# Weight words by ScalarE, dilated heads in three tiles of 128 rows, and a new order list in an attention and feed-forward kernel

## The chip, the core and the metric

The kernel runs on one core of one Trainium2 chip. The metric is the device time of one execution in microseconds; the time of a kernel is the median of its runs. Five engines work beside one another, each through its own list of instructions: TensorE (PE, with PEld for its weight loads), VectorE (DVE), ScalarE (ACT), GpSimd (POOL) and SyncE (SP), whose list here issues nearly all transfers between HBM and on-chip memory.

## The reference

Two stages, one behind the other. Attention over 8 batches, 8 heads, 576 positions and a head dimension of 64, in which each query sees at most 32 keys: in heads 0 to 3 ("plain") the 32 latest positions, in heads 4 to 7 ("dilated") 32 positions at a distance of 4.

```python
mask_plain = (rel >= 0) & (rel < 32)
mask_dil = (rel >= 0) & (rel < 128) & (rel % 4 == 0)
attn = softmax(where(mask, q @ k.T / sqrt(64), -1e9))     # + 1e-9 in the denominator
x = (attn @ v).transpose(0, 2, 1, 3).reshape(4608, 512)
h = x @ w_in                                              # 512 -> 2048
out = (h * tanh(log1p(exp(h)))) @ w_out                   # 2048 -> 512
```

All arrays are float32, and the matrices arrive as pairs of 32-bit words.

## The kernel before, in words

**Units.** The work is cut into 16 units, a batch and a half of its positions each: 288 tokens, all eight heads. For each unit the attention's output x is written transposed into one tile of 512 rows in four chunks and multiplied by both matrices. Matrices, x and the gated values are split into a high and a low fp16 part, and products of parts are summed in PSUM.

**Direct units and late units.** Units 0 to 2 are "direct": their attention runs in float32, the probabilities and x are transposed by TensorE (`transpose_p` L659, `transpose_x` L738), and the second matrix is multiplied in full by `ff2` (L972). Units 3 to 15 are "late": probabilities and values are split in fp16 parts (three passes), transposed by DMA, and the second matrix goes through a scheme with seven products in place of eight (`product`, L933, 144 columns). The first matrix is `ff1` (L790, 288 columns) in all units; Mish is an activation into `hm` and a few operations of ScalarE and VectorE.

**Attention on TensorE.** Queries are cut into blocks of 32, and a block meets only its window of 64 keys (32 before it and its own), so each small matmul uses 64 rows by 32 columns of TensorE. Plain heads: three tiles of three blocks, on 96 partitions. Dilated heads: the positions of each of the four residues modulo 4 are a tile of three blocks that overlap a little, on 96 partitions, thus four tiles. `scores_of_kind` (L577) writes scores of one kind of head, `scores` subtracts maxima, `exps` takes the exponential, `values` (L689) multiplies by v with a column of ones for the denominator. The four dilated tiles don't fit into one PSUM bank at once, so `values` runs for them twice, `va.1` and `va.2`, with two tiles each, and `transpose_x` as well.

**Weights.** Each matrix is loaded in groups (`w_load`; in the list `wl`), as words in four buffers `raw`. `w_max` (`wm`) copies the high words for the maximum: by ScalarE for w_in, by GpSimd for w_out (the set `BY_POOL`). `w_words` (`ww`) builds float32 from the two words in three steps: a scaled low half by GpSimd (L411), then two word operations of VectorE (L413, L415). `w_scale` (`ws`) finds a power of two with matmuls by a matrix of ones, and `w_split` (`wp`) makes the high part by ScalarE (L422) and the low part by VectorE (L424).

**Order.** Every engine's order is fixed by one list, `ORDER`. Each word names a step and its unit or group (`ld1` the loads of q and k of unit 1, `lv1` of its v, `qp1` GpSimd's copy of its q, `sp` scores, `sc` maxima, `ex`, `tp`, `va`, `tx` as above, `pr` scales of v, `ff0.6` a chunk of ff1, `fo` of ff2, `fs` scales of ff1). A step is a generator: each time its word comes up, the part up to the next `yield` is issued. "=2" names the PSUM bank, of four, that the step takes. `kw` and `kh` are matmuls whose result nobody reads. In `loads_v` of a direct unit the dilated v comes in one transfer for each third of a residue (`vd`, 128 KB); they write parts of one tile, and each waits on SP for the one ahead of it.

Of the kernel before, what the change touches and what calls it, by code (L numbers as in the profile page):

```python
# [51 lines left out]
ww1.1.0 pr1 va1.2 ff0.2 ww0.2.0 va1.2 va1.0 ws0.2=3 ww0.2.0 ff0.2 ff0.3=1 ws0.2 tx1.2=2 ld2 tx1.2 ff0.3 wp0.2.0
va1.0 wp0.2.1 tx1.0=3 tx1.2 wp0.2.0 wp0.2.1 sp2.1=0 wm1.1.0 va1.1=2 sp2.1 ff0.3 wl1.1.1 va1.1 tx1.0 tx1.0 ff0.5=1
ww1.1.1 va1.1 sc2.1 ff0.4=3 wm1.1.1 qp2 ft wl1.0.0 wl1.0.1 fs0.4 fs0.2 va1.1 ww1.1.0 wm1.0.0 ff0.5 ff0.4 tx1.1=0 fs1
sp2.0=2 ff0.5 ww1.1.1 tx1.1 tx1.1 ff0.4 sp2.0 gt0.0=0 ff1.0=1 gt0.1=1 lv2 sc2.0 ws1.1=0 ww1.1.1 ww1.0.0 ff1.6=3
ws1.1 lv2 ff1.7=2 ex2.0 ff1.7 wp1.1.1 wp1.1.1 gt0.2=2 gt0.0 ff1.0 ff1.2=0 gt0.3=3 gt0.3 ld3 ex2.1 ff1.6 wm1.0.1 lv2
# [1005 lines left out]
```

## Time and profile before

| what | value |
|---|---|
| median of 3 runs | 858.7 us (857.71 to 860.95) |
| the profiled execution | 862.81 us, of which the profile's span is 860.9 |
| mean granted clock of TensorE | 0.992 |
| TensorE busy | 842.1 us (98% of the span) |
| VectorE busy | 636.1 us (74%) |
| ScalarE busy | 477.8 us (55%) |
| GpSimd busy | 96.0 us (11%) |
| read and written in HBM | 56.89 MB and 9.44 MB |

The span begins at the first and ends at the last instruction of the program; the rest of the profiled execution's own time lies around it. Busy time is the union of an engine's instructions. The matmuls' ends are modelled, so a busy TensorE says that it had matmuls in flight, not that it worked at its peak.

### The profile page before, as it was taken

Reading aid. Unit: us, or ns where it says so; the run is one execution under the profiler, and the core shown is the slowest. Engines: PE = TensorE matmul, PEld = TensorE weight load, DVE = VectorE, ACT = ScalarE, POOL = GpSimd, SP = SyncE. Lnnn points to the kernel's source line nnn. Section 1 sums busy time; section 2 is a strip of 40 time slices with the busy share of each in tenths; the row PEclk is TensorE's granted clock in tenths of the full one; section 3 lists DMA queues with packets and bytes.
Section 4 is the critical chain, followed back from the end, with each engine's and each line's share of the span. In section 5 each row is a group of like instructions: output and inputs, shape, how many; then the busy total and the mean of one; then the engine's idle time right before and its main releaser. Section 6 shows DMA issues by size and latency. Waiting matters only on the chain.

```text
span 860.9 us, 32197 instructions
## 1 busy us (share of the span) xinstructions
PE 842.1 (98%) x14818; PEld 727.3 (84%) x14821; DVE 636.1 (74%) x818; ACT 477.8 (55%) x615; POOL 96.0 (11%) x99
## 2 busy tenths in 40 slices
PE   8798999999999999999999999999999999999998
PEld 7486777788788998988999889988889889988898
DVE  3788998586999897968777587977878764854353
ACT  2464655453486558765753775766446656624342
POOL 5116583210010001000000000010000000000000
PEclk9989999999999999999999999999999999999999
DMA  8648543366320437253623373725335160421001
GB/s 270 213 151 266 154 146 87 73 144 130 70 57 13 126 80 178 57 144 96 126 67 102 69 150 76 131 72 102 94 73 109 43 127 18 57 40 34 1 22 37
DMA packets 154887, 86.29 MB, mean 100 GB/s; under 512 B 92288, under 2 KB 150656, under 8 KB 154752
## 3 DMA queue, kind: packets, MB, share of 16 engines
q1 hardware_dynamic: 154752, 84.24, 40.9%
q8 instruction: 116, 1.90, 1.0%
q14 instruction: 19, 0.16, 0.1%
HBM read 56.89 MB, written 9.44 MB: 77 GB/s over the span
## 4 chain that ended last, share of the span: by engine, by line
PE 86%; DMA 7%; DVE 3%; SPq 2%; ACT 1%; issue 1%; POOL 0%; DVEq 0%; POOLq 0%; ACTq 0%
PE b L790 40%; PE b L933 31%; PE b L972 8%; DMA vf<-in_vd 4%; PE b L689 4%; PE b L577 3%; DMA raw<-in_w_in 2%; DMA knd<-in_kdT 1%; DVE g L903 1%; SPq L348 1%; DVE hm L909 0%; DVE w L424 0%; SPq L501 0%; PE b L385 0%; ACT g L901 0%
## 5 line engine op out<-in xcount | busy, mean ns | idle before, releaser
L790 PE MATMUL b<-x,w 128*128 128x288 f16 x3072 | 393.4, 286 | 0.2 <-ACT hm L796 0.2
L790 PEld LDWEIGHTS <-w 128*128 128x128 f16 x3072 | 295.4, 98 | 75.5 <-issue 0.6
L903 DVE SCALAR_TENSOR_TENSOR g<-hm,sg,g 128x1152 f16<-128x1152 f32 (+1 forms) x104 | 131.3, 1272 | 53.7 <-ACT g L901 52.9
L933 PE MATMUL b<-g,w 128*128 128x144 f16 x2496 | 164.9, 226 | 0.8 <-issue 0.7
L933 PEld LDWEIGHTS <-w 128*128 128x128 f16 x2496 | 158.4, 98 | 3.2 <-issue 1.1
L796 ACT ACTIVATE hm<-b,fs 128x576 f32<-128x576 f32 x128 | 92.8, 738 | 113.5 <-PE b L790 99.2
L901 ACT ACTIVATE g<-hm,sg 128x1152 f16<-128x1152 f32 (+1 forms) x104 | 116.0, 1127 | 40.1 <-PE b L933 26.4
L481 POOL COPY qp<-qn 128x576 f32<-128x576 f32 x15 | 34.9, 2326 | 433.6 <-DMA qn<-in_qT 317.9
L909 DVE TENSOR_TENSOR hm<-hm 128x576 f32<-128x576 f32 x104 | 79.0, 763 | 1.9 <-ACT hm L796 0.4
L972 PE MATMUL b<-g,w 128*128 128x288 f16 x576 | 73.3, 286 | 0.1
L947 ACT ACTIVATE y<-b,fo 128x288 f32<-128x288 f32 x52 | 40.6, 786 | 58.9 <-PE b L933 57.6
L972 PEld LDWEIGHTS <-w 128*128 128x128 f16 x576 | 55.6, 98 | 14.4 <-DVE w L424 0.3
L952 DVE SCALAR_TENSOR_TENSOR y<-b,fo,y 128x144 f32<-128x144 f32 x78 | 33.6, 478 | 45.8 <-PE b L933 22.7
L933 PE MATMUL b<-g,g 128*128 128x144 f16 x936 | 66.6, 226 | 0.3 <-DVE y L952 0.2
L933 PE MATMUL b<-g,late_sums 128*128 128x144 f16 x936 | 65.9, 226 | 0.0
L933 PEld LDWEIGHTS <-g 128*128 128x128 f16 x936 | 60.6, 98 | 2.2 <-issue 0.6
L933 PEld LDWEIGHTS <-late_sums 128*128 128x128 f16 x936 | 60.0, 98 | 0.5
L727 ACT CAST x<-xs 96x512 f16<-96x512 f32 (+1 forms) x39 | 26.7, 686 | 30.9 <-DMA x<-x 17.1
L729 DVE TENSOR_TENSOR x<-xs,x 96x512 f16<-96x512 f32 (+1 forms) x39 | 30.1, 772 | 16.6 <-ACT x L727 16.4
L545 DVE SCALAR_TENSOR_TENSOR vh<-vn,s,vh 128x2688 f16<-128x2688 f32 (+1 forms) x13 | 35.2, 2705 | 8.6 <-ACT vh L543 8.6
L705 DVE TENSOR_TENSOR xs<-b,rec 96x512 f32<-96x512 f32 (+1 forms) x48 | 37.2, 776 | 4.4 <-DVE rec L703 0.5
L689 PEld LDWEIGHTS <-pT 64*32 64x32 f16 (+1 forms) x3276 | 30.2, 90 | 5.3 <-issue 3.6
(127 smaller groups left out, 821.1 us busy)
## 6 DMA issues: line engine op xcount, KB each, us to landing
qn<-in_qT SPq DMA_DIRECT2D x15, 576.0 KB, 5.3
vn<-in_vd SPq DMA_DIRECT2D x66, 128.0 KB, 3.8
raw<-in_w_out SPq DMA_DIRECT2D x16, 512.0 KB, 5.2
out_T<-y SPq DMA_DIRECT2D x26, 288.0 KB, 2.8
raw<-in_w_in SPq DMA_DIRECT2D x12, 512.0 KB, 7.4
vn<-in_v SPq DMA_DIRECT2D x14, 288.0 KB, 4.2
knd<-in_kdT SPq DMA_DIRECT2D x14, 224.0 KB, 4.7
vn<-in_v SPq DMA_DIRECT2D x12, 256.0 KB, 3.7
```

What stands on the lines that cost most here:

```text
L481: nc.gpsimd.tensor_copy(qp.rearrange("p (b r i) -> p b r i", r=NR, i=SQ // NR), d["q"][:, :2 * HT].rearrange("p (b i r) -> p b r i", r=NR, ...
L545: nc.vector.scalar_tensor_tensor(lo, src, s, hi, ALU.mult, ALU.subtract)
L689: nc.tensor.matmul(avv[s * SQ:(s + 1) * SQ, a, t - t0, h * (D + 1):(h + 1) * (D + 1)], p, vv[vi][ks, v0:v0 + D + 1], start=(i == 0), stop= ...
L705: nc.vector.tensor_tensor(xs.rearrange("p (a t h e) -> p a t h e", a=2, h=2, e=D), avv[:, :, :, 1:AW - 1].rearrange("p a t (h e) -> p a t ...
L790: nc.tensor.matmul(ph[:, h, :HT], w1[j][:, c, wi, k * P:(k + 1) * P], x_of(d, xi, c), start=(n == 0), stop=(n == len(seq) - 1))
L796: nc.scalar.activation(d["m"][p][:, half, k0:k0 + 2], ph[:, :, :HT], AF.Mish, scale=d["fs"][:, j:j + 1])
L901: nc.scalar.activation(hi, src, AF.Identity, scale=sg)
L903: nc.vector.scalar_tensor_tensor(lo, src, sg, hi, ALU.mult, ALU.subtract)
L909: nc.vector.tensor_tensor(a, a, b, op=op)
L933: nc.tensor.matmul(acc[e], left(l, e, p, wi)[:, k * P:(k + 1) * P], right(gi, k), start=(n in opens and p == 0 and q == 0), stop=(last and ...
L947: nc.scalar.activation(into(half, t), by(acc), AF.Identity, scale=fo)
L972: nc.tensor.matmul(po[:, :HT], w2[:, e, j, wi, k * P:(k + 1) * P], d["g"][j][:, gi, k, :], start=(j == 0 and n == 0), stop=(j == NCH - 1 a ...
```

## The change

It does three things. The scaled low halves of all weight words and the copies for the maxima of w_out are made by ScalarE (`BY_POOL` is empty), none by GpSimd. The twelve dilated blocks of a unit lie in three tiles of four blocks, on 128 partitions, in place of four tiles of three on 96; `block` gives the residue and the third for a tile's place j, the tiles' widths follow from `QS` and `NB`, and one `values` and one `transpose_x` per kind remain (`va0.1`, `tx0.1`; there is no `va0.2`). And `ORDER` is a new list throughout, in which the same steps stand in another order and with other banks. Below, its first lines stand for the list.

```diff
 ORDER = """
-ld0 ld0 wl0.3.0 lv0 mf cs0 qp0 ww0.3.0 xa0 cs1 wl0.3.1 xa1 kw18 kh32 sp0.0=0 wm0.3.0 ld0 mf lv0 ww0.3.0 ld0 wm0.3.0
-wl0.0.0 wm0.3.1 lv1 ww0.3.0 sp0.0 wl0.0.1 ww0.3.0 ww0.3.1 kw17 sp0.1=1 sc0.0 ww0.0.0 sp0.1 ww0.3.0 ww0.3.1 lv0
-ww0.3.1 ws0.3=2 sc0.1 wm0.0.0 ws0.3 lv0 ww0.0.0 ww0.3.0 ld1 ww0.0.1 ww0.0.0 sc0.0 sc0.1 wm0.0.1 ex0.0 ld1 wp0.3.1
-kw8 tp0.0=3 ww0.0.1 wp0.3.1 kw1 ws0.0=2 ex0.1 ld1 ws0.0 ww0.0.1 qp1 wp0.0.0 tp0.1=0 kw3 sp1.0=1 tp0.1 sp1.0 ld1 lv0
-sp1.1=2 sp1.1 lv1 wp0.0.1 wl0.1.0 tp0.0 wp0.0.0 sc1.0 sc1.0 sc1.1 pr0 sc1.1 pr0 va0.0=0 wl0.1.1 wp0.3.0 pr0=3 pr0
-ex1.1 va0.0 va0.1=3 ww0.1.0 va0.0 wp0.3.0 va0.1 ex1.0 va0.2=2 lv1 va0.2 lv1 va0.0 va0.1 tp1.1=1 va0.1 wl0.2.1
-wm0.1.0 va0.2 fs0.0 tx0.1=3 va0.0 va0.2 wm0.1.1 tp1.1 kw1 tx0.0=0 ww0.1.0 tx0.1 ww0.1.1 lv1 tx0.0 tp1.0=2 ww0.1.1
-tp1.0 tx0.2=1 tx0.1 wl0.2.0 ws0.1=2 tx0.2 tx0.0 ld2 tx0.2 ww0.2.1 ff0.6=3 ff0.6 wp0.0.1 ws0.1 wm0.2.1 ww0.1.1
...
+wl0.3.0 wl0.3.1 lv0 ww0.3.0 kw12 wm0.3.0 wl0.0.0 ww0.3.0 wm0.3.0 lv0 cs0 ld0 wl0.0.1 ww0.3.0 wm0.3.1 wm0.0.0 ld0
+kh30 mf ww0.0.0 qp0 ld0 ww0.3.1 kw4 ww0.0.0 mf ld0 kw26 ww0.3.0 ww0.3.0 ww0.3.1 ws0.3=0 ww0.0.0 cs1 sp0.0=1 sp0.0
+ws0.3 sp0.1=2 wm0.0.1 sp0.1 ww0.0.1 ld1 xa1 qp1 lv0 lv0 ww0.0.1 sc0.0 sc0.0 ld1 ww0.3.1 ld1 sc0.1 ex0.0 ws0.0=3
+sc0.1 tp0.0=0 ex0.1 tp0.0 sp1.0=1 ld1 kw2 lv2 lv0 ws0.0 sp1.1=3 sp1.1 ww0.3.0 wp0.0.0 ww0.0.1 wp0.0.1 tp0.1=2 sc1.1
+wp0.3.0 sc1.1 wp0.3.0 wp0.3.1 wl0.1.1 va0.0=0 va0.0 pr0 tp0.1 pr0 sp1.0 va0.0 sc1.0 pr0=2 pr0 xa0 sc1.0 va0.1=2
+va0.1 va0.0 wp0.0.0 ex1.1 va0.1 va0.1 va0.0 va0.1 kw2 wl0.2.0 ex1.0 tx0.0=3 lv1 ww0.2.0 ld2 tx0.1=0 ld2 tx0.0
+wm0.2.0 tx0.1 tp1.0=1 qp2 wl0.1.0 wp0.0.1 wp0.3.1 tx0.0 ww0.1.1 lv1 wl0.2.1 tp1.1=2 lv1 wm0.1.0 tx0.1 ww0.1.0
+wm0.1.1 ff0.6=3 tp1.1 ff0.0=0 ww0.2.0 ff0.0 fs0.0 ww0.2.0 ff0.0 tp1.0 ww0.1.1 ww0.1.0 ff0.6 ws0.1=2 ff0.1=0 ff0.7=1
+ww0.1.0 lv1 ws0.1 fs0.3 wm0.2.1 ww0.1.1 ff0.1 ww0.2.1 ww0.2.1 wp0.1.0 ff0.6 wp0.1.0 ws0.2=2 ff0.7 wl1.0.0 sp2.0=3
...
-    NB = (NPB, NR)
+    NB = (NPB, NR * NS * SQ // P)
+    QS = (QB, P)
...
-    XW = 4 * HT + 4 * NR * QB
+    XW = 4 * (QS[0] * NB[0] + QS[1] * NB[1])
+    QMAX = max(QS)
+    GMAX = max(NB)
...
-    BY_POOL = {(1, g) for g in range(NCH)}
+    BY_POOL = set()
...
-    ident_b = const.tile([QB, QB], BF16, name="ident_b")
+    ident_b = const.tile([QB, 2 * QB], BF16, name="ident_b")
...
-            nc.gpsimd.tensor_scalar(lo[:, c], lo[:, c].bitcast(U32), LOW_SCALE, LOW_BIAS, ALU.mult, ALU.add)
+            nc.scalar.activation(lo[:, c], lo[:, c].bitcast(U32), AF.Copy, scale=LOW_SCALE, bias=LOW_BIAS)
...
+    def block(kind, t, j):
+
+        return divmod(t * P // SQ + j, NS) if kind else (t, j)
...
             for a in range(2):
-                for s in range(NS):
-                    k0 = a * (NR * d["kd"] if kind else d["kw"]) + key_of(d, kind, t, s)
-                    q0 = (2 + a) * HT + t * RB + s * DQ if kind else a * HT + t * QB + s * SQ
+                for j in range(nq // SQ):
+                    r, s = block(kind, t, j)
+                    k0 = a * (NR * d["kd"] if kind else d["kw"]) + key_of(d, kind, r, s)
+                    q0 = (2 + a) * HT + r * RB + s * DQ if kind else a * HT + t * QB + s * SQ
                     for h in range(2):
                         hs = slice(h * D, (h + 1) * D)
-                        c = (2 * t + a) * WK
+                        c = (2 * t + a) * w
                         q = d["q"] if kind else d["qp"]
-                        nc.tensor.matmul(pt[s * SQ:(s + 1) * SQ, h, c:c + w], q[hs, q0:q0 + SQ], d["k"][kind][hs, k0:k0 + w],
+                        nc.tensor.matmul(pt[j * SQ:(j + 1) * SQ, h, c:c + w], q[hs, q0:q0 + SQ], d["k"][kind][hs, k0:k0 + w],
                                          start=not d["direct"], stop=True, skip_group_check=True)
...
+        nb, w, nq = NB[kind], width_of(d, kind), QS[kind]
         n = 2 * nb
-        sb = d["sb", kind] = pool.tile([QB, 2 * NR * 2 * WK], F32, name="sb", bufs=2)
-        nm = pool.tile([QB, 2, 2 * NR], F32, name="nm", bufs=4)
-        src = pt[:QB, :, :n * WK].rearrange("p h (g k) -> p h g k", k=WK)[:, :, :, :w]
+        sb = d["sb", kind] = pool.tile([QMAX, 2 * GMAX * 2 * WK], F32, name="sb", bufs=2)[:nq]
+        nm = pool.tile([QMAX, 2, 2 * GMAX], F32, name="nm", bufs=4)[:nq]
+        src = pt[:nq, :, :n * w].rearrange("p h (g k) -> p h g k", k=w)
...
-    def span(p):
-
-        return (1, 2 * p - 2, 2 * p) if p else (0, 0, NPB)
-
-    def values(u, p):
-        d = U[u]
-        kind, t0, t1 = span(p)
+                nc.tensor.transpose(pt[:, h, t * nq:(t + 1) * nq], sb[:, g * P:(g + 1) * P], ident[:nq, :nq])
+        pp = d["p", kind] = early.tile([P, 2, nb * nq], F32, name=f"pp{kind}")
+        yield
+        nc.scalar.copy(pp, pt[:, :, :nb * nq])
+
+    def values(u, kind):
+        d = U[u]
         pp = d["p", kind]
-        nb, ng = NB[kind], 2 * (t1 - t0)
+        nb, nq = NB[kind], QS[kind]
         av = take("b", banks)
-        avv = av[:QB, :, :ng * (D + 1)].rearrange("p a (t e) -> p a t e", e=AW)
+        avv = av[:nq, :, :nb * AW].rearrange("p a (t e) -> p a t e", e=AW)
         vv = d["vh"]
         passes = [(None, 0)] if d["direct"] else [(0, 1), (0, 0), (1, 0)]
-        for t in range(t0, t1):
+        for t in range(nb):
             for h in range(2):
                 for i, (pi, vi) in enumerate(passes):
-                    for s in range(NS):
+                    for j in range(nq // SQ):
                         for a in range(2):
                             ks = slice(a * WK, a * WK + width_of(d, kind))
-                            v0 = window(d, kind, t, s) * VW + h * (D + 1)
+                            v0 = window(d, kind, *block(kind, t, j)) * VW + h * (D + 1)
                             if d["direct"]:
-                                p = pp[ks, h, t * QB + s * SQ:t * QB + (s + 1) * SQ]
+                                p = pp[ks, h, t * nq + j * SQ:t * nq + (j + 1) * SQ]
                             else:
-                                c = ((pi * 2 + h) * nb + t) * QB + s * SQ
+                                c = ((pi * 2 + h) * nb + t) * nq + j * SQ
                                 p = pp[ks, c:c + SQ]
-                            nc.tensor.matmul(avv[s * SQ:(s + 1) * SQ, a, t - t0, h * (D + 1):(h + 1) * (D + 1)], p,
+                            nc.tensor.matmul(avv[j * SQ:(j + 1) * SQ, a, t, h * (D + 1):(h + 1) * (D + 1)], p,
...
-    def transpose_x(u, p):
-        d = U[u]
-        kind, t0, t1 = span(p)
-        nt = t1 - t0
-        xs = d.pop(("xs", kind, t0)).rearrange("p (a t k) -> p a t k", a=2, k=P)
+    def x_span(d, kind):
+
+        c = 4 * QS[0] * NB[0]
+        return d["x"][:, c:] if kind else d["x"][:, :c]
+
+    def transpose_x(u, kind):
+        d = U[u]
+        nb, nq = NB[kind], QS[kind]
+        xs = d.pop(("xs", kind)).rearrange("p (a t k) -> p a t k", a=2, k=P)
         if not d["direct"]:
 
-            x16 = take("x16", x16s)[:, :4 * nt * P]
-            form = "p (t i a k) -> p i a t k" if kind else "p (i a t k) -> p i a t k"
-            hi, lo = (x16.rearrange(form, i=2, a=2, k=P)[:, i] for i in range(2))
+            x16 = take("x16", x16s)[:nq, :4 * nb * P]
+            hi, lo = (x16.rearrange("p (i a t k) -> p i a t k", i=2, a=2, k=P)[:, i] for i in range(2))
             nc.scalar.copy(hi, xs)
             yield
             nc.vector.tensor_tensor(lo, xs, hi, op=ALU.subtract)
             yield
-            dst = x_span(d, kind, t0, t1)
-            nc.sync.dma_start_transpose(dst.rearrange("k (g q) -> k g q", q=QB), x16)
+            nc.sync.dma_start_transpose(x_span(d, kind).rearrange("k (g q) -> k g q", q=nq), x16)
...
-        ap = x[:, (2 * i + a) * QB:]
-        return bass.AP(ap.tensor, ap.offset, [list(ap.ap[0]), [4 * QB, NR], [SQ + SD - DQ, NS], [1, SD]])
+        ap = x[:, at0:]
+        return bass.AP(ap.tensor, ap.offset, [list(ap.ap[0]), [NS * SQ, NR], [SQ + SD - DQ, NS], [1, SD]])
```

## Rows read from the trace of the kernel before

**Rows 1.** Windows: us; busy us (instructions) of PE, PEld, DVE, ACT, POOL; clock; DMA; GB/s

```profile
0.00:50.00 50.00, 41.14 (x707) 32.51 (x710) 29.38 (x43) 21.66 (x30) 16.94 (x38) 0.90 0.69 215
50.00:86.00 36.00, 33.19 (x551) 25.39 (x553) 30.03 (x45) 16.98 (x28) 14.12 (x9) 0.95 0.77 240
86.00:140.00 54.00, 51.84 (x713) 41.98 (x702) 50.39 (x70) 32.29 (x41) 36.24 (x17) 1.00 0.41 123
140.00:840.00 700.00, 698.91 (x12597) 610.63 (x12595) 519.08 (x653) 402.13 (x514) 28.66 (x36) 1.00 0.39 85
```

**Rows 2.** The chain that ended last, 259 to 305 us: start, length, what

```profile
259.02 2.94 PE b L790 x24
...
301.93 2.74 DVE g L903 x2
```

**Rows 3.** The chain that ended last, the first 50 us

```profile
12.50 10.20 DMA vf<-in_vd
26.54 5.98 DMA vf<-in_vd
36.00 8.72 DMA vf<-in_vd
44.74 2.75 DMA vf<-in_vd
```

**Rows 4.** Timeline of PE: start, length, instruction, [idle before and its releaser]

```profile
42.98 1.57 PE L689 MATMUL b<-vf,pp 64*32 64x65 f32 x73 [3.33 <-issue]
...
50.66 2.61 PE L790 MATMUL b<-x,w 128*128 128x288 f16 x20
...
86.20 1.64 PE L790 MATMUL b<-x,w 128*128 128x288 f16 x12
```

**Rows 5.** DMA issues: operation xcount, KB each, median us from issue to landing

```profile
qn<-in_qT SPq DMA_DIRECT2D x15, 576.0 KB, 5.3
...
vf<-in_vd SPq DMA_DIRECT2D x14, 128.0 KB, 2.8
```

**Rows 6.** VectorE by shape, 0 to 160 us: busy, mean ns | idle

```profile
L424 DVE SCALAR_TENSOR_TENSOR w<-raw,ws,w 128x1024 f16<-128x1024 f32 x14 | 20.8, 1495 | 2.4 <-ACT w L422 2.4
...
L323 DVE TENSOR_REDUCE m<-vf 128x1 bf16<-128x1024 f32 x4 | 4.7, 1210 | 0.0
...
L705 DVE TENSOR_TENSOR xs<-b,rec 96x768 f32<-96x768 f32 x3 | 2.9, 954 | 0.1
...
L424 DVE SCALAR_TENSOR_TENSOR w<-w,ws,w 128x1024 f16<-128x1024 f32 x2 | 2.6, 1276 | 0.0
...
L703 DVE RECIPROCAL rec<-den 96x12 f32<-96x12 f32 x3 | 0.6, 214 | 0.4 <-ACT den L697 0.4
...
L531 DVE TENSOR_REDUCE m<-b 128x1 f32<-128x2 f32 x3 | 0.5, 154 | 0.8 <-PE b L330 0.8
```

**Rows 7.** Groups of GpSimd and ScalarE by shape, 0 to 160 us

```profile
L368 POOL TENSOR_SCALAR w<-raw 128x1024 f32<-128x1024 f32 x8 | 26.6, 3329 | 2.8 <-DMA raw<-in_w_out 2.5
L411 POOL TENSOR_SCALAR raw<-raw 128x1024 int32<-128x1024 uint32 x13 | 16.5, 1270 | 42.4 <-DMA raw<-in_w_in 14.0 <-DMA raw<-in_w_out 13.6 <-DVE w L415 10.2
...
L370 ACT ACTIVATE w<-raw 128x1024 f32<-128x1024 f32 x5 | 5.7, 1131 | 17.4 <-DMA raw<-in_w_in 17.4
```

**Rows 8.** Small matmuls: two rows of PE's timeline, then groups of PE by shape

```profile
354.51 1.13 PE L577 MATMUL b<-knd,qn 64*32 64x56 f32 x96
...
444.25 1.35 PE L689 MATMUL b<-vh,pT 56*32 56x65 f16 x144
...
L738 PE MATMUL b<-ident,xs 96*128 96x96 f32 x42 | 5.9, 277 | 0.0
...
L689 PE MATMUL b<-vh,pT 64*32 64x65 f16 x2412 | 24.8, 196 | 0.0
```

**Rows 9.** Waits, 0 to 160 us: instruction and releaser: us in total, times, longest

```profile
ACT w L370 <- DMA raw<-in_w_in: 23.7, 7, 6.2
...
POOL raw L411 <- DMA raw<-in_w_in: 16.4, 4, 8.5
```

More of the change, by code (lines that the diff above doesn't have):

```diff
@@ L52 @@
[L52 to L56, printed above, removed]
@@ L290, in constants @@
         if i == 0:
-            nc.scalar.copy(ident_b, ident[:QB, :QB])
+            nc.scalar.copy(ident_b.rearrange("p (c i) -> p c i", c=2), ident[:QB, :QB].unsqueeze(1).broadcast_to([QB, 2, QB]))
         else:
@@ L296, in masks_late @@
     def masks_late():
-        pm = take("b", banks)[:QB, 0, :NPB * WK]
+        pm = take("b", banks)
+        pk = pm[:, 1, :2 * NB[1] * WK].rearrange("p (f t k) -> p f t k", f=2, k=WK)
+        pm = pm[:QB, 0, :NPB * WK]
         nc.tensor.matmul(pm, ident_p, m_b[:, :NPB * WK], start=True, stop=True)
+        for t in range(NB[1]):
+            nc.tensor.matmul(pk[:, :, t], ident_b[:, t * SQ:t * SQ + P],
+                             m_b[:, 3 * WK:5 * WK].rearrange("p (f k) -> p f k", f=2), start=True, stop=True)
         yield
-        m_p.extend(late.tile([QB, 2 * NPB * WK], BF16, name=f"m_p{i}") for i in range(2))
-        nc.scalar.copy(m_p[0].rearrange("p (t a k) -> p t a k", a=2, k=WK),
+        m_p.extend([late.tile([QS[k], 2 * NB[k] * WK], BF16, name=f"m_p{k}{i}") for i in range(2)] for k in range(2))
+        nc.scalar.copy(m_p[0][0].rearrange("p (t a k) -> p t a k", a=2, k=WK),
                        pm.rearrange("p (t k) -> p t k", k=WK).unsqueeze(2).broadcast_to([QB, NPB, 2, WK]))
-        nc.scalar.copy(m_p[1].rearrange("p (a k) -> p a k", k=WK),
+        nc.scalar.copy(m_p[0][1].rearrange("p (a k) -> p a k", k=WK),
                        pm[:, WK:2 * WK].unsqueeze(1).broadcast_to([QB, 2 * NPB, WK]))
+        yield
+        for f in range(2):
+            w = WK if f else WD
+            nc.scalar.copy(m_p[1][f][:, :2 * NB[1] * w].rearrange("p (t a k) -> p t a k", a=2, k=w),
+                           pk[:, f, :, :w].unsqueeze(2).broadcast_to([P, NB[1], 2, w]))
     w1 = [const.tile([P, NCC, 2, CH], F16, name=f"w1{g}") for g in range(NCH)]
@@ L603, in scores @@
             for h in range(2):
-                nc.tensor.matmul(pt[:QB, h, :n * w].rearrange("p (g k) -> p g k", k=w), ident[:QB, :QB],
-                                 nm[:, h, :n].unsqueeze(2).broadcast_to([QB, n, w]), start=False, stop=True,
+                nc.tensor.matmul(pt[:nq, h, :n * w].rearrange("p (g k) -> p g k", k=w), ident[:nq, :nq],
+                                 nm[:, h, :n].unsqueeze(2).broadcast_to([nq, n, w]), start=False, stop=True,
                                  skip_group_check=True)
@@ L619, in exps @@
         else:
-            nc.scalar.activation(x, x, AF.Exp, bias=ln_p[:QB])
+            nc.scalar.activation(x, x, AF.Exp, bias=ln_p[:QS[kind]])
     p16s, x16s, pTs = [], [], []
@@ L639, in transpose_p @@
         sb = d.pop(("sb", kind))
-        nb, w = NB[kind], width_of(d, kind)
+        nb, w, nq = NB[kind], width_of(d, kind), QS[kind]
         n = 2 * nb
@@ L651, in transpose_p @@
             pT = pTs[kind]
-            nc.sync.dma_start_transpose(pT.rearrange("k (g q) -> k g q", q=QB), p16s[kind][:, :2 * n * P])
+            nc.sync.dma_start_transpose(pT.rearrange("k (g q) -> k g q", q=nq), p16s[kind][:, :2 * n * P])
             d["p", kind] = pT
@@ L692, in values @@
             yield
[L693 to L694 removed]
+        dn, rc = (pool.tile([QMAX, 2, GMAX, 2], F32, name=n, bufs=3)[:nq, :, :nb] for n in ("den", "rec"))
         if d["direct"]:
[L697 removed]
+            nc.scalar.activation(dn, avv[:, :, :, ::AW - 1], AF.Identity, scale=d["f_v"][:nq], bias=d["eps"][:nq])
         else:
@@ L730, in transpose_x @@
             yield
-            dst = x_span(d, kind, t0, t1)
-            nc.sync.dma_start_transpose(dst.rearrange("k (g q) -> k g q", q=QB), x16)
+            nc.sync.dma_start_transpose(x_span(d, kind).rearrange("k (g q) -> k g q", q=nq), x16)
             return
         px = take("b", banks)
-        for t in range(nt):
-            for a in range(2):
-                o, i = (t, a) if kind else (a, t)
-                nc.tensor.transpose(px[:, o, i * QB:(i + 1) * QB], xs[:, a, t], ident[:QB, :QB])
+        for a in range(2):
+            for t in range(nb):
+                nc.tensor.transpose(px[:, a, t * nq:(t + 1) * nq], xs[:, a, t], ident[:nq, :nq])
         yield
-        dst = x_span(d, kind, t0, t1)
-        form = "p (o i n) -> p i o n" if kind else "p (i o n) -> p i o n"
-        hi, lo = (dst.rearrange(form, o=2, i=2)[:, i] for i in range(2))
-        src = px[:, :, :(nt, 2)[kind] * QB]
+        hi, lo = (x_span(d, kind).rearrange("p (i a n) -> p i a n", a=2, i=2)[:, i] for i in range(2))
+        src = px[:, :, :nb * nq]
         nc.scalar.copy(hi, src)
```

295 lines of the change are left out of this document (140 added, 155 removed).

## Prediction

> **What bounds the kernel now.** I read the windows first, cut where the kind of work changes. In the 700 us from 140 to 840 TensorE is busy for 698.91 us and so idles 1.1 us [rows 1]. A stretch of full-size matmuls runs at a fixed pace: 24 of 288 columns in 2.94 us, 122.5 ns each [rows 2]. So from 140 us to the end the time is the list of matmuls itself, and the change takes none of the full-size ones away. VectorE (519 of 700 us) and ScalarE (402) have slack there. What can move is (a) the front, before 86 us, (b) the small matmuls of attention, which stand between the large ones, and (c) the few waits.
>
> The front is not a TensorE limit. The first full-size matmul starts at 50.66 us and the first of the second unit at 86.20 [rows 4]. Before 50 us the engine is busy 41 us, but part of that is the keep-warm matmuls, and the granted clock is 0.90 [rows 1]. The chain of waits shows who sets this stretch: transfers into vf, one behind the other [rows 3]. SP issues in order, and each residue's piece of a unit's v waits for the piece before it to land, so everything behind it on SP waits too: 10.20 us from 12.50, 5.98 from 26.54, 8.72 from 36.00, 2.75 from 44.74. Unit 0's v is complete at about 36.0, when VectorE can take its maximum.
>
> **The change, part by part.**
>
> *Order of the loads.* The new list sends four blocks of weights (2 MB) before anything else, and unit 0's q and k behind six to eight transfers of weights. Scores of unit 0 will start at some 22 us in place of 10. That costs nothing by itself: values cannot start before unit 0's v is there, and between scores and values a kind needs a maximum, a subtraction, an exponential and a copy, so the two kinds need eight passes, at most about 1 us each (954 ns for 768 columns) [rows 6]: 8 us, an estimate. When does v land? Ahead of the first vd piece stood 576 + 288 + 2048 + 160 + 256 + 160 + 2048 + 128 = 5664 KB (q and vd as in [rows 5]; weights, k and v by the sizes of their tiles in the code); it landed at 22.69. Now unit 1's q (576 KB) stands ahead of it as well: 0.59 MB at the 0.3 MB a us that the first 20 us move (5.8 MB by 22.7 less some 3 us of start and landing) is 2 us more. In the next link, 1856 KB in 9.8 us, the same 576 KB are missing, 2 us less. So the last link begins at 32.5 as now, and v is there at 36.0 as now.
>
> Behind it VectorE has a fixed queue in the new list until the first full-size matmul's operand exists: two maxima of v (2 x 1.21), the maximum of unit 1's plain scores (0.95, as for any 768 columns), the five small ones of prep (5 x 0.154), low halves of three weight blocks (3 x 1.28), two quotients (2 x (0.95 + 0.21)), low parts of x (0.95 for 768 columns and, for 576, three quarters of it, 0.72): 12.0 us [rows 6]. With the few tens of ns between instructions the first full-size matmul starts at 48.3, against 50.66: 2.4 us. Now TensorE had waited 3.33 us before 42.98 in this stretch [rows 4], which is where the old list lost it.
>
> From there 13 halves of ff1 (1.47 each), two weight maxima and unit 2's plain scores stand before unit 1's values: 22.5 us, to 70.8, and about 1 us for the bank that waits for the first Mish and its table load. Unit 1's v lands at: 3936 KB of weights, q2 and k2, 288 and 1024 KB, all behind 32.5, together 4.0 + 1.3 MB, at 0.3 MB a us 18 us, 50; then four links at 2.8 us [rows 5] and two legs of 6 us between them (as from 26.54) [rows 3], 73. So a wait of 1 to 2 us, another 2.4 for the two maxima that prep of unit 1 needs, then 3 halves and small work: unit 1's ff1 starts at 83 against 86.20. I take 3 us for the front; bounds 6 (all of the idle time behind 50 us goes) and -3 (each of the two landings 3 us later than worked out).
>
> *Low halves and maxima from GpSimd to ScalarE.* GpSimd loses the eight maxima of w_out, 3.33 us each, and seventeen low halves, thirteen of them at 1.27; ScalarE gains these 25 instructions at 1.13 us (the two half-size ones count half), 27 us [rows 7]. It was busy 71 of the first 140 us [rows 1], so it comes to 70% there and by its sum stays below VectorE. VectorE gains: its low half of a weight takes 1495 ns in the form that runs beside GpSimd and 1276 in the other [rows 6], 14 x 0.22 = 3 us. VectorE is busy 50.39 of 54 us in 86 to 140 [rows 1], TensorE idles 2.2 there, so I count 0.5 us for it, bounds 0 and 2.
>
> *Dilated heads in three tiles of 128 partitions.* VectorE and ScalarE work on three quarters of the columns: 1024 to 768 at about 1 ns a column, seven passes a unit on VectorE, 1.8 us a unit, 23 us in 13 units. It lies beside TensorE's 698.91 of 700 us and costs or gives nothing there, except near 300 us, where the chain of waits runs through VectorE for a few us [rows 2]; 0.5 us, bounds 0 and 1.5. The transposes through the DMA carry the same bytes, x in two issues a unit in place of three, hidden as well.
>
> On TensorE the number of small matmuls stays: 96 records of scores and 144 of values a unit, in eight positions (two of 64 rows by four of 32 columns) in place of six. Would more positions be faster? Values: 144 in 1.35 us, less one latency of 0.20, 8.0 ns apart [rows 8]. At the pace of the large ones (122.5 ns for 288 columns) 65 columns stream in 28 ns, which six positions would allow every 4.6 ns. The row is at nearly twice that, so something other than the positions sets it, and eight change nothing. Scores: 96 dilated ones in 1.13, less the same latency, 9.7 ns apart [rows 8]. That is above 8.0, so positions may bind here. Bounds: nothing, and three quarters (0.91 to 0.68), 0.23 x 13 = 3.0 us. I take down to 8.0 ns, 0.15 a unit, and as some of it is start and mode change, 1.5 us in all. Direct units: two transposes fewer of 14 on each side, and per transpose some 0.14 us (5.9 us of 42, overlapping less than those of full size) [rows 8], so 0.28 a side and unit, 0.6 for the two sides of the one unit whose attention lies behind the front.
>
> The Trainium skill, TensorEngine Tiling (Array Packing), Tiling Modes, lists 64x32 as eight tiles that load and multiply independently of each other. By that, both groups would take three quarters: 0.23 + 0.29 a unit. The trace's 8.0 ns speaks against it for the values.
>
> Sum: 3 + 0.5 + 0.5 + 1.5 + 0.6 = 6.1 us. The profiled execution took 862.81 (span 860.9 and 1.9 around it), 4.1 above the median of the runs; from the median, 858.7 - 6.1 = **852.6**. A change of under 0.5% (4.3 us) is what a measurement of this kernel cannot tell from none.
>
> **Rivals.** *Eight positions pay in full* (0.14): values are bound by positions too, 0.52 us a unit, 6.8 in place of 1.5, 847.3. For it: scores are slower than values at the same six positions. Against: the 4.6 ns above.
>
> *The front gives nothing* (0.26): unit 1's v comes later than the 73 worked out, and every us later is a us of TensorE; without the 3 us, 855.6. For it: four links of that chain in [rows 3] took 2.75 to 10.20 us, so a landing is known to a few us only.
>
> *ScalarE waits where GpSimd waited* (0.14, slower). GpSimd's low halves waited 16.4 us for landings of one matrix, ScalarE's maxima 23.7 [rows 9]; behind GpSimd's stood only its own copies of q. In the new list the blocks of the second and third weight group stand ahead of Mish of ff1 on ScalarE, and a bank is given back by Mish. Place: the block that is issued last before unit 1's v, and the first of w_out. A wait as long as the link of 10.20 us, less the 2.94 us that the halves into another bank cover [rows 2], is 7.3 us; two of them, 867.2. It decides from 10.4 us in all (852.6 to 863.0). Against: the 4.0 MB behind 32.5 need 13.4 us at 0.3 MB a us and some 2 of landing, 48, and by the sum of its passes in the new list ScalarE comes to that block at 47, an estimate.
>
> **Chances.** Forecast 0.46 (its own range 848 to 854.3), eight positions 0.14, front without gain 0.26, ScalarE 0.14. Faster by over 0.5%: the first two, 0.60; within 0.5%: 0.26; slower: 0.14. From 844 (front 6 and positions in full, less the unknown) to 861 all but the last and a little of the second lie inside.
>
> **What would show it.** Right: v of unit 0 read by VectorE near 36, first full-size matmul near 48, unit 1's near 83, 140 to 840 still full, GpSimd's weight groups gone, VectorE's low halves all near 1.28. Dilated scores near 1.0 and values near 1.35 a unit. Wrong: waits of TensorE for Mish (ScalarE for raw), values near 1.05, a first full-size matmul later than 50.7, new waits in 140 to 840.

## The result, and the profile after

The changed kernel takes 864.23 us (median of 9 runs, 860.68 to 869.65) against 860.07 for the kernel before (9 runs): a ratio of 1.0053, 95% interval 1.0027 to 1.0078. It is slower by about half a per cent; the forecast was 852.6, in a range of 844 to 861. The profiled execution took 869.65 us, the longest of the nine, with a span of 867.6; a second profile of the same kernel (the first experiment) stands beside it.

Windows of the changed kernel, columns as in [rows 1]:

```profile
0.00:50.00 50.00, 37.97 (x679) 28.82 (x680) 22.81 (x36) 20.16 (x26) 14.20 (x33) 0.80 0.71 222
50.00:86.00 36.00, 33.08 (x475) 25.43 (x474) 29.55 (x42) 29.46 (x39) 1.23 (x1) 0.99 0.71 193
86.00:140.00 54.00, 49.44 (x659) 40.32 (x660) 41.94 (x59) 40.57 (x49) 1.22 (x1) 0.97 0.44 137
140.00:840.00 700.00, 697.55 (x12636) 607.46 (x12634) 496.92 (x617) 389.95 (x490) 23.80 (x40) 1.00 0.42 85
```

GpSimd's weight work is gone and VectorE has lost 22 us behind 140 us, as forecast, and TensorE still idles only 2.4 us there. The loss stands ahead of it: TensorE is busy 3.2 us less in the first 50 us, at a granted clock of 0.80 in place of 0.90, and 2.4 us less between 86 and 140.

TensorE's timeline of the changed kernel, as in [rows 4]:

```profile
17.97 0.58 PE L389 MATMUL b<-w,ones 128*128 128x512 bf16 x1 [3.23 <-DVE w L420]
...
24.96 0.80 PE L573 MATMUL b<-m_b,ident_b 96*128 96x128 bf16 x6 [2.72 <-POOL m_b L273]
...
31.62 2.47 PE L615 MATMUL b<-nm,ident 128*128 128x384 f32 x4
...
40.14 1.56 PE L615 MATMUL b<-nm,ident 128*128 128x384 f32 x4 [0.77 <-DVE nm L611]
...
54.24 6.04 PE L787 MATMUL b<-x,w 128*128 128x288 f16 x48 [1.19 <-DVE x L743]
...
83.30 0.42 PE L695 MATMUL b<-vf,pp 64*32 64x65 f32 x19 [0.71 <-issue]
...
91.39 0.41 PE L593 MATMUL b<-knd,qn 64*32 64x64 f32 x18 [2.80 <-issue]
```

The first full-size matmul starts at 54.24 us, 3.6 later than before and 5.9 later than forecast. Two things are to be seen ahead of it. TensorE waits 2.72 us at 22 for the dilated mask `m_b` that GpSimd makes. And the same four matmuls of a maximum take 2.47 us at 31.6 and 1.56 at 40: in the 12 us behind 20 the granted clock is 0.50, the lower of the two levels (1.2 GHz), after the 3.23 us without work before 17.97. What these two cost is tried below. Further on stand two waits that the profile calls "issue", 0.71 and 2.80 us, each in the middle of a group of small matmuls.

VectorE's timeline of the changed kernel says when unit 0's v is read:

```profile
36.23 0.69 DVE L396 TENSOR_REDUCE wm<-b 128x1 f32<-128x512 f32 x1 [7.92 <-PE b L996]
...
41.58 1.29 DVE L431 SCALAR_TENSOR_TENSOR w<-raw,ws,w 128x1024 f16<-128x1024 f32 x1 [1.49 <-ACT w L429]
42.78 2.34 DVE L330 TENSOR_REDUCE m<-vf 128x1 bf16<-128x1024 f32 x2
```

The two maxima of v (L330) start at 42.78, though the last piece of v was issued at 32.6 and landed 2.7 us later, at about 35.2 (forecast 36.0). Ahead of them in VectorE's queue stands a weight's maximum that waited 7.92 us for a keep-warm matmul (L996): the list has `kw2` between the matmuls of `ws0.0`, which end near 31.8, and their reading, and all of TensorE's work up to `kw2` has to pass first.

### The profile page after: what moved, and what is told of

The parts are those of the page before. It is cut to its first block, busy times and chain, and to the rows that moved or that the text cites. A ratio compares the mean times of both kernels' runs of the same rounds, so it can differ in the third digit from the quotient of the medians.

```text
span 867.6 us, 32051 instructions
## 1 busy us (share of the span) xinstructions
PE 841.6 (97%) x14818; PEld 725.4 (84%) x14818; DVE 605.7 (70%) x770; ACT 489.5 (56%) x610; POOL 40.5 (5%) x74
## 4 chain that ended last, share of the span: by engine, by line
PE 80%; DVE 7%; issue 4%; ACT 4%; DMA 3%; POOL 1%; SPq 1%; DVEq 0%; POOLq 0%; ACTq 0%
PE b L787 37%; PE b L930 29%; PE b L969 6%; PE b L695 3%; PE b L593 3%; DVE g L900 1%; DMA vf<-in_vd 1%; PE b L615 1%; DMA raw<-in_w_out 1%; ACT g L898 1%; DMA vn<-in_v 1%; DVE nm L611 1%; ACT vh L550 1%; DMA vn<-in_vd 1%; POOL m_b L270 1%
## 5 line engine op out<-in xcount | busy, mean ns | idle before, releaser
L488 POOL COPY qp<-qn 128x576 f32<-128x576 f32 x15 | 22.5, 1503 | 447.2 <-DMA qn<-in_qT 363.1
L552 DVE SCALAR_TENSOR_TENSOR vh<-vn,s,vh 128x2688 f16<-128x2688 f32 (+1 forms) x13 | 35.2, 2708 | 10.9 <-issue 6.9
L609 DVE SCALAR_TENSOR_TENSOR sb<-b,m_p 96x768 f32<-96x768 f32 (+2 forms) x26 | 24.1, 928 | 14.6 <-PE b L593 14.2
L695 PE MATMUL b<-vh,pT 64*32 64x65 f16 (+1 forms) x3276 | 32.4, 197 | 0.2 <-DMA pT<-p 0.2
L708 DVE TENSOR_TENSOR xs<-b,rec 96x768 f32<-96x768 f32 (+1 forms) x32 | 30.6, 956 | 2.8
```

The source lines that it names most:

```text
L552: nc.vector.scalar_tensor_tensor(lo, src, s, hi, ALU.mult, ALU.subtract)
L695: nc.tensor.matmul(avv[j * SQ:(j + 1) * SQ, a, t, h * (D + 1):(h + 1) * (D + 1)], p, vv[vi][ks, v0:v0 + D + 1], start=(i == 0), stop=(i == ...
L708: nc.vector.tensor_tensor(xs.rearrange("p (a t h e) -> p a t h e", a=2, h=2, e=D), avv[:, :, :, 1:AW - 1].rearrange("p a t (h e) -> p a t ...
```

## The experiments

Two theories at first. **A, the front:** the new list's order of instructions in the first 50 us is at fault. **B, ScalarE:** its waits for landings stand ahead of what TensorE needs. A third, **F**, came out of the second round. Ratios are to the kernel before on the same chip.

**The changed kernel again** (no edit).

> The changed kernel once more, for a second profile. Theory A: the loss lies in the front of the new list and is there in every execution. The maximum of unit 0's dilated scores waits for the mask that GpSimd makes only behind its copy of q (about 23 to 25 us), TensorE idles some 3 us before 18 us and is at the lower clock to 35, and a weight's maximum is read only behind keep-warm matmuls (about 36 us): first full-size matmul 52 to 55 us, time 862 to 866. The 2.80 us gap near 88.6 us and the lower clock behind it are then the part that differs from one execution to the next. Rival C: the profiled execution was an outlier in its front too: this one starts full-size matmuls at 51 us or earlier.

865.92 us, ratio 1.0070 (1.0054 to 1.0086), span 863.4. The first full-size matmul starts at 53.27; the mask is waited for again (2.83 us). The two "issue" waits are there as well, at the same instructions: they belong to the kernel, not to one execution.

```profile
82.85 0.41 PE L695 MATMUL b<-vf,pp 64*32 64x65 f32 x19 [1.82 <-issue]
...
89.26 0.41 PE L593 MATMUL b<-knd,qn 64*32 64x64 f32 x18 [1.97 <-issue]
```

**Words and maxima by ScalarE alone**, on the old list and tiles.

```diff
-    BY_POOL = {(1, g) for g in range(NCH)}
+    BY_POOL = set()
...
-            nc.gpsimd.tensor_scalar(lo[:, c], lo[:, c].bitcast(U32), LOW_SCALE, LOW_BIAS, ALU.mult, ALU.add)
+            nc.scalar.activation(lo[:, c], lo[:, c].bitcast(U32), AF.Copy, scale=LOW_SCALE, bias=LOW_BIAS)
```

> The kernel before, its list and its tiles, with only the low halves and the maxima of w_out on ScalarE. Theory A: nothing of the loss comes from here, 858 to 862 (ratio 0.998 to 1.002). Rival B: ScalarE's waits for weights that land late stand before the denominators and Mish, so 863 or more (ratio above 1.003), with waits of ScalarE for in_w_out in front of a denominator or of Mish.

869.71 us, ratio 1.0122 (1.0101 to 1.0143): B, on this list. ScalarE's timeline of this kernel, and TensorE's:

```profile
63.51 1.10 ACT L411 ACTIVATE raw<-raw 128x1024 int32<-128x1024 uint32 x1 [5.71 <-DMA raw<-in_w_in]
```

```profile
68.17 2.50 PE L689 MATMUL b<-vf,pp 64*32 64x65 f32 x120 [5.98 <-ACT hm L796]
```

The low half waits 5.71 us for its words, Mish behind it comes late, no bank is free, and unit 1's values wait 5.98 us. That is the mechanism of the slower rival.

**The new list and tiles, words and maxima back on GpSimd** (the same two lines reversed in the changed kernel).

> The changed kernel with its new list and tiles, but low halves and maxima of w_out back on GpSimd. Theory A: the front stays as in the changed kernel up to the first full-size matmul (53 to 57 us, as GpSimd also has the mask and the copies of q to make), time 862 to 868. Rival B: with ScalarE free of the words it is faster than the changed kernel, 861 or less.

871.55 us, ratio 1.0136 (1.0107 to 1.0165): 5.6 us slower than the changed kernel, not faster, and more than A's 862 to 868. TensorE waits 8.16 us for VectorE's words, and these wait for GpSimd:

```profile
23.11 0.58 PE L389 MATMUL b<-w,ones 128*128 128x512 bf16 x1 [8.16 <-DVE w L420]
```

The first full-size matmul is at 55.84, in A's 53 to 57. So each list fits its own engine for the words, and the changed kernel doesn't lose by leaving them to ScalarE.

**Three dilated tiles alone** (the tiles of the change, words and maxima on GpSimd), with the old list; `va.1` and `tx.1` take the places of the old second passes.

```diff
-... va3.1=3 ... va3.1 ... va3.1 va3.1 ... va3.2=3 ... va3.2 ... va3.2 ... va3.2 ...
+... va3.1=3 ... va3.1 va3.1 ... va3.1 ... va3.1 ...
```

> The kernel before and its list, with only the dilated heads in three tiles of four blocks (values and transposes of the dilated heads at the places of the old second pass; low halves and maxima of w_out on GpSimd as before). Theory A: 856 to 860 (ratio 0.995 to 1.000), dilated values of a late unit at 1.28 us, as in two passes of 0.68 together less 0.08, dilated scores at 1.06 to 1.10. Rival: the tiles hold values back (one bank for all of them, a longer group at the end), 861 or more.

887.91 us, ratio 1.0326 (1.0301 to 1.0351), far above A's 856 to 860; the rival's 861 or more is met, but not by what the rival named. Between 140 and 840 us TensorE idles 21 us, most of it in waits that no engine releases. The longest, in TensorE's timeline:

```profile
345.22 2.08 PE L692 MATMUL b<-vh,pT 56*32 56x65 f16 x218
352.08 0.52 PE L692 MATMUL b<-vh,pT 64*32 64x65 f16 x34 [4.77 <-issue]
```

Values of two kinds now stand back to back, over 200 small matmuls in a row, and then TensorE stops for 4.77 us inside the group.

**Three edits of the new list's front.** First the mask step one place ahead of the copy of q:

```diff
-... kh30 mf ww0.0.0 qp0 ld0 ww0.3.1 kw4 ww0.0.0 mf ld0 kw26 ...
+... kh30 mf ww0.0.0 mf qp0 ld0 ww0.3.1 kw4 ww0.0.0 ld0 kw26 ...
```

> The changed kernel, its list with GpSimd's second mask step one place ahead of its copy of unit 0's q, nothing else. Theory A (the front's instruction order): the 2.7 us that TensorE waits for m_b near 22 us go, first full-size matmul 50.5 to 52 us, time 1.5 to 3 us below the changed kernel. Rival (the landing of unit 1's v sets the end of the front): the first full-size matmul is as early, but the time stays within 1 us of the changed kernel, with a wait of TensorE before unit 1's values in its place.

861.27 us, ratio 1.0023 (1.0009 to 1.0036), 3 to 5 us below the changed kernel: A, with more than the 1.5 to 3 us expected. The mask is ready at 8.4 us and the first full-size matmul starts at 48.85:

```profile
48.85 6.04 PE L785 MATMUL b<-x,w 128*128 128x288 f16 x48 [1.02 <-DVE x L741]
```

Then, on the changed kernel, more keep-warm matmuls in the gap before 17 us (`kw38` for `kw26`):

> The changed kernel with 12 more keep-warm matmuls behind the 26 (kw38 for kw26), so that TensorE is busy to 17 us, nothing else. Theory A: the granted clock stays at its upper level behind 17 us, the two groups of 4 matmuls of the maxima (2.9 and 2.5 us) and the weight maximum (1.9 us) fall to 1.6 and 1.0, first full-size matmul 50 to 51.5 us, time 2 to 4 us below the changed kernel. Rival: the clock falls all the same in the 2.7 us wait for the mask, first full-size matmul 53 to 54, no change.

873.07 us, ratio 1.0169 (1.0148 to 1.0190): 7 to 9 us slower than the changed kernel, which neither side expected. The first full-size matmul is at 53.54, as the rival says, since the mask is waited for all the same (2.91 us); and that although the granted clock between 20 and 32 us is 0.67 to 0.82 in place of 0.50. The loss is far from the edit: new "issue" waits at 220.65 (1.10 us), 309.50 (1.14), 572.45 (0.93) and more, where the list is unchanged.

Both edits:

> Both of these edits. Theory A: the two add up, first full-size matmul 48.5 to 50 us, 3 to 5 us below the changed kernel, about level with the kernel before. Rival (unit 1's v): first full-size matmul as early, time at most 1 us below the changed kernel.

868.70 us, ratio 1.0121 (1.0098 to 1.0144), first full-size matmul at 48.93: A's place for it (48.5 to 50), not A's time, for the late waits are there. From 12 to 36 us the granted clock is 1.00 here; with the mask edit alone it is 0.55 and 0.59 from 16 to 24, and the first full-size matmul is as early (48.85). So the lower clock from 16 to 24 us costs nothing that shows at that matmul; what it costs from 24 to 32, where it is 1.00 in both, these two don't tell.

And with the two keep-warm matmuls behind the reading of the weight's maximum:

```diff
-... sp1.0=1 ld1 kw2 lv2 lv0 ws0.0 sp1.1=3 ...
+... sp1.0=1 ld1 lv2 lv0 ws0.0 kw2 sp1.1=3 ...
```

> Both edits, and the two keep-warm matmuls that stand between a weight's maximum and its reading behind the reading. Theory A: VectorE reads that maximum near 30 us in place of 36, the maximum of unit 0's v moves to its landing near 36, first full-size matmul 47.5 to 49 us (the 48.3 of the prediction), 4 to 7 us below the changed kernel. Rival (unit 1's v): the time stays at most 1 us below the changed kernel and TensorE waits 3 us or more before unit 1's values or their scales.

866.88 us, ratio 1.0093 (1.0069 to 1.0117). The first full-size matmul is at 47.30, 6.9 us earlier than in the changed kernel's first profile, and the kernel is no faster. There is no wait of 3 us before unit 1's values or scales as the rival had; the loss is again in the late part.

**Theory F.** What the three kernels with `kw38` have in common is the count of TensorE's instructions ahead of its real work: 12 more `kw` are 24 matmuls and 24 weight loads. The page of the changed kernel:

```profile
PE 841.6 (97%) x14818; PEld 725.4 (84%) x14818; DVE 605.7 (70%) x770; ACT 489.5 (56%) x610; POOL 40.5 (5%) x74
...
q8 instruction: 116, 1.90, 0.9%
```

14818 matmuls and as many weight loads, with 58 rows of other kinds, are 29694 instructions; over 116 packets of the queue q8 that is 256 a packet. So q8 brings TensorE's instructions, 256 at a time. I then counted, for packet i of each trace, how many instructions TensorE had begun when it landed, less 256 i. In the 14 profiles this is never above 449. At every "issue" wait of 0.5 us or more, in all of them, TensorE stopped with 446 to 450 begun and went on 1.2 to 1.8 us after a packet's landing (at the one of 0.71 us above the packet landed at 418, and TensorE still ran to 450). So TensorE can run to about 450 of this count and then stops until the next block is there. A packet starts no earlier than 155 instructions into that count, and lands 2.2 to 2.4 us after that point in the median behind 140 us, but as late as 8.7 and 7.9 us after it between 55 and 140 us in the changed kernel's two profiles, where weights are loading. Both are the second of two blocks that TensorE came to within 4 us; with three tiles alone such a second block lands 9.3 us after that point at 356 us, where no weights load any more. Large matmuls take 122.5 ns a pair of instructions [rows 2], small ones some 8, so 450 - 155 instructions last 18 us of the one and 1.2 of the other: a long row of small matmuls at the wrong place of a block stops TensorE.

```
kernel                packets that landed at 440 or above, behind 140 us    TensorE idle, 140 to 840 us
before                0                                                     1.09
changed               0 (highest 417)                                       2.45
front edits, kw38     4                                                     7.65
tiles alone           8                                                     21.25
```

Stops of this kind are in the kernel before too, one of them late, where a packet landed at 430:

```profile
18.30 1.28 PE L577 MATMUL b<-knd,qn 64*32 64x64 f32 x52 [1.95 <-issue]
...
34.38 0.44 PE L577 MATMUL b<-qk 64*32 64x64 f32 x23 [1.30 <-issue]
...
357.34 3.79 PE L933 MATMUL b<-g,w 128*128 128x144 f16 x58 [0.71 <-issue]
```

With the tiles alone the block edges have hardly moved: 1435 instructions of TensorE stand ahead of the first full-size matmul, 1431 before. There it is the rows, longer and back to back, that reach the edges.

The Trainium skill, Runtime: NRT & Kernel Launch, Instruction fetch mechanics, describes blocks of 256 instructions, fetched through a queue of the engine's own while the block before is executed, and calls the cost of a block's edge mostly hidden. The traces agree on the 256 and the queue; the stops here are not hidden.

**The front edits with the changed kernel's count of instructions.**

```diff
-kh30 mf ww0.0.0 mf qp0 ld0 ww0.3.1 kw4 ww0.0.0 ld0 kw38 ...
+mf ww0.0.0 mf qp0 ld0 ww0.3.1 kw4 ww0.0.0 ld0 kw41 ...
```

> The kernel of the third front edit with another mix of keep-warm matmuls (kw41 for kw38, the short kh30 left out), so that TensorE executes exactly as many instructions before its real work as in the changed kernel; in the kernels with kw38 they were 48 more. Everything else as there. Theory F (instructions are fetched in blocks of 256, and where a burst of small matmuls meets the edge of a block TensorE stops until the next block lands): the stops in the late part (1.1 to 1.8 us near 212, 301, 564, 629, 654 us) go again, idle and slow steps behind 140 us fall by 6 to 7 us, time 858 to 861, the first full-size matmul at 47 to 48 us as there. Rival: the earlier front itself brings the late waits, time 865 to 868 as there.

859.29 us, ratio 1.0003 (0.9987 to 1.0019), 7.6 us below the kernel with `kw38`. Windows of that kernel, then of this one:

```profile
140.00:840.00 700.00, 692.35 (x12594) 602.35 (x12593) 489.83 (x606) 385.32 (x485) 24.48 (x40) 1.00 0.40 85
```

```profile
0.00:50.00 50.00, 41.84 (x738) 34.46 (x739) 30.89 (x43) 27.64 (x34) 12.14 (x33) 0.97 0.86 265
...
140.00:840.00 700.00, 697.77 (x12713) 609.83 (x12711) 495.99 (x616) 390.24 (x490) 24.36 (x40) 1.00 0.42 85
```

The late idle time falls from 7.65 to 2.23 us by a mix of keep-warm matmuls at 10 us; the order of the work is the same. Both kernels start unit 1's ff1 at 84.6 us, so that all of the difference lies behind it: it is not the earlier front that brings the late waits.

**The kernel before with 96 more instructions** (`kh80` for `kh32`, 48 short matmuls at the start).

> The kernel before with 48 more short keep-warm matmuls at its start (kh80 for kh32): 96 instructions of TensorE more, some 2.2 us of work in a place where unit 0's v is still some 20 us away. Theory F: the late part's bursts meet block edges that they did not meet before, stops of 1 to 2 us at 5 or more places behind 140 us, 5 to 12 us above the kernel before (865 to 872). Rival: instructions are fetched far enough ahead, time within 1.5 us of the kernel before.

892.19 us, ratio 1.0379 (1.0356 to 1.0401): F, at 32 us where 5 to 12 were expected. The first full-size matmul is not late (50.12). Between 140 and 840 us TensorE idles 23.37 us, and packets landed at 440 or above 11 times. One such place in its TensorE's timeline:

```profile
288.31 1.05 PE L686 MATMUL b<-vh,pT 64*32 64x65 f16 x108
289.25 0.89 PE L574 MATMUL b<-knp,qp 64*32 64x64 f32 x67
292.57 0.31 PE L574 MATMUL b<-knp,qp 64*32 64x64 f32 x5 [2.44 <-issue]
```

108 values and 67 scores, 350 instructions in under 2 us, and a stop five matmuls before the end of the group. The expectation had stops of 1 to 2 us at 5 places or more; the trace has 14 behind 140 us, of 0.5 to 3.0 us.

**The two stops behind unit 1.** In the new list they remain. Their place is the same in each kernel of it with the unchanged count (those with `kw38` have one, of 2.6 to 4.4 us). Here they are in the timeline of the front edits with the unchanged count:

```profile
75.83 0.42 PE L693 MATMUL b<-vf,pp 64*32 64x65 f32 x19 [1.55 <-issue]
...
83.34 0.41 PE L591 MATMUL b<-knd,qn 64*32 64x64 f32 x18 [3.07 <-issue]
```

From the second stop's end to the span's end it is 857.2 - 83.34 = 773.9 us here, 859.2 - 84.85 = 774.4 with the mask edit alone, 863.4 - 89.26 = 774.1 in the changed kernel's second profile, and 867.6 - 91.39 = 776.2 in its first (with a clock of 0.61 from 92 to 96). But for the 2 us of that first profile, what happens ahead of that stop is all that tells these kernels apart. So I moved the scores behind 12 large matmuls:

```diff
-... sp2.1=1 ff0.4 tx1.0 ww1.0.0 gt0.2=1 sp2.1 ... ex2.0 sc2.1 gt0.2 ... wm1.1.1 ff1.3=0 ww1.1.0 ...
+... sp2.1=1 ff0.4 tx1.0 ww1.0.0 gt0.2=1 ... ex2.0 gt0.2 ... wm1.1.1 ff1.3=0 sp2.1 sc2.1 ww1.1.0 ...
```

> The kernel above, and the last third of unit 2's dilated scores (32 small matmuls) and their maximum behind the next 12 large matmuls of ff1, nothing else. Theory F: the stop of some 2 us inside those scores (near 83 us) shrinks below 0.7, time 1 to 2 us below the kernel above. Rival: the stop is a wait for data of the scores, and TensorE stops as long at their new place; no change.

859.49 us, ratio 0.9998 (0.9988 to 1.0009). The stop left the scores, as F says; the block is now waited for 0.96 us in the weight matmuls behind them. But the time did not fall: the block lands at 81.59 us in place of 81.87, so its stop ends only 0.3 us earlier, at 83.00, wherever the scores stand. And I let x pass a weight's low half on VectorE:

```diff
-... wl0.1.0 wp0.0.1 wp0.3.1 tx0.0 ... wm0.1.0 tx0.1 ww0.1.0 ...
+... wl0.1.0 wp0.3.1 tx0.0 ... wm0.1.0 tx0.1 wp0.0.1 ww0.1.0 ...
```

> The kernel with the three front edits and the unchanged count of TensorE's instructions, and VectorE's low half of one more weight block (which the first chunk of ff1 does not read) behind the two low parts of x that the first chunk reads; no instruction of TensorE is added or moved. Theory A: the first full-size matmul starts 1.2 us earlier (the 1.28 us of the low half), and the time falls by as much, to about 858. Rival: the front's gain is given back at the two stops of TensorE near 75 and 82 us, where the next block of instructions lands no earlier because weights are loading: they grow by what the front gained, time within 0.5 us of that kernel (859.3).

860.19 us, ratio 1.0019 (1.0000 to 1.0037). TensorE's timeline:

```profile
43.44 0.41 PE L785 MATMUL b<-x,w 128*128 128x288 f16 x2
44.28 1.89 PE L785 MATMUL b<-x,w 128*128 128x288 f16 x12 [0.43 <-ACT x L739]
46.47 4.34 PE L785 MATMUL b<-x,w 128*128 128x288 f16 x34 [0.30 <-DVE w L429]
```

The first two full-size matmuls start at 43.44 and the next at 44.28, 1.5 us earlier than the 45.74 of the kernel above, but 34 of these 48 then wait for the low half that was moved, which the next chunk reads, and the 48 end 1.0 us earlier. The first stop takes another 0.4 of that (1.94 us against 1.55), since its block lands only 0.7 us earlier, and the second stop ends at 82.79, 0.55 earlier. That is the rival's way for a part of the gain; the second stop did not grow (1.41 against 3.07).

## Why the prediction was wrong

**The front: the step that failed.** It worked out when unit 0's v lands, and what VectorE does behind that landing; it took for granted that VectorE is free when v lands. The landing was right (35.2 us, forecast 36.0), and so was the length of the queue behind it. With the front mended and the count unchanged, v's maxima start at 34.02 us and the first full-size matmul 11.7 us later (12.0 forecast):

```profile
34.02 2.34 DVE L328 TENSOR_REDUCE m<-vf 128x1 bf16<-128x1024 f32 x2
```

```profile
45.74 6.04 PE L785 MATMUL b<-x,w 128*128 128x288 f16 x48 [2.02 <-DVE x L741]
```

In the changed kernel the same chain, 11.5 us long, starts at 42.78, since two things stand ahead of it that the prediction never priced: the mask behind GpSimd's copy of q, and `kw2` ahead of a reading. That scores start at some 22 us costs nothing by itself, as the prediction said: in the mended front they start at 19.26, and the first full-size matmul is early. What the list puts between the scores and v is what costs. The term was -2.4 us at the first full-size matmul and measured +3.6 and +2.6 in the two profiles. The edit of the mask alone is worth 4.4 us there (53.27 to 48.85; the clock, too, is back at 1.00 from 24 us on with it) and 3 to 5 us of the kernel's time; the place of `kw2` is worth 1.6 us there (48.93 to 47.30).

**No term for instruction blocks.** The 3.33 us before 42.98 [rows 4] were read as what the old list lost and the new one would save. "Issue" is time in which the engine waited for nothing that the profile shows, and the packet count stands at 448 there: a stop for instructions. The new list has none at that place and two behind unit 1, 3.5 us in the first profile and 3.8 in the second. So a mended front is not a gain either: the first full-size matmul at 45.74 is 2.6 us ahead of the forecast's, unit 1's ff1 starts at 84.6 (83 forecast), and the time is 859.29 against 859.98 for the kernel before. The two stops take 4.6 us there; that they alone hold the gain back is not shown, as no kernel of the new list is without a stop there. From the first full-size matmul to the end the forecast gained 3.7 us (6.1 less 2.4); measured is 813.4 and 810.1 against 810.2. And 1.4 us of the miss lie in the start: the forecast went from 858.7, and the kernel before has a median of 860.07 over nine runs.

**Dilated heads.** Eight positions change nothing, scores less than forecast and values as forecast. Two late groups of the changed kernel, to be held against [rows 8]:

```profile
231.64 1.35 PE L695 MATMUL b<-vh,pT 56*32 56x65 f16 x144
...
439.96 1.13 PE L593 MATMUL b<-knd,qn 64*32 64x56 f32 x96
```

The same 1.13 and 1.35 us: the term of 1.5 us is nothing, the rival of full payment (0.90 and 1.06) is out (less the latency of 0.20 the scores took 0.93, not the 0.91 of the prediction), and something other than the positions sets the pace of the scores as well, which are 9.7 ns apart as before. What the tiles do change is the length of a row: two passes of 72 have become one of 144, nearer to a block. With the old list, where they also come to stand beside the plain values, this showed as 21 us of idle time.

**Words by ScalarE.** The changed kernel's group of VectorE's low halves, 0 to 160 us, to be held against [rows 6]:

```profile
L431 DVE SCALAR_TENSOR_TENSOR w<-raw,ws,w 128x1024 f16<-128x1024 f32 x14 | 17.9, 1290 | 7.5 <-ACT w L429 7.5
```

It fell from 1495 to 1290 ns, as forecast from the other form's 1276, and GpSimd's weight groups are gone. No gain of TensorE from the 2.9 us is seen: from 86 to 140 us it idles 4.6 us, before 2.2. The slower rival exists where the list doesn't fit (words alone, 10.3 us), and on the new list the move is worth 5.6 us; so it was neither the forecast's 0.5 nor the rival's loss; that rival named the right side by luck, since its cause, ScalarE's waits, is not what made the kernel slower.

**What held.** 140 to 840 us stayed full (2.45 us idle, before 1.09). This was read from the trace of before, and has a condition that the prediction did not know: both lists lie so that, but for the 0.71 us at 357.34, no late group meets a block's edge. That was luck, as the runs with a few dozen instructions more show.

## What to carry to other kernels

When work is moved earlier or later in an in-order program, follow each engine's queue ahead of the critical step too, not only behind it: a mask or a spare matmul can hold the engine that the landing was worked out for. A wait called "issue" inside a group of small matmuls is to be counted in instructions: from the edge of a block of 256 some 450 can begin before the next block must have landed. In a kernel with many small matmuls any edit that changes TensorE's count of instructions moves all later block edges, so compare variants at an equal count, or the comparison measures that; where an edit makes rows longer, as the tiles did, even an equal count is not enough.

## What the runs showed of the hardware

I had not expected that 48 instructions at 10 us could cost 7.6 us, all of it behind 84 us, nor that 96 could cost 32; that an instruction block can land 8.7 us after it could first start (that loading weights is the reason is not shown: 9.3 us were seen without it, and both were the second of two blocks in quick succession); and that a group of small matmuls keeps its pace, 8.0 ns apart for values and 9.7 for scores, whether six or eight positions of the array are in use.
